# Decode kernel on one core: K and V in transfers of four batches, P^T by 32x32 transposes, w3 earlier, w4 in six pieces

## The chip, the core and the metric

The kernel runs on one core of a Trainium2 chip, alone. The metric is device time in microseconds. The core has TensorE (PE, with its weight loads listed apart as PEld), VectorE (DVE), ScalarE (ACT), GpSimd (POOL) and SyncE (SP), and 16 DMA engines that all queues share. In this kernel SP issues nearly every transfer.

## What is computed

The reference, cut to what matters (all data bf16, B = 4, one query position, D = 576, 32 query heads and 16 kv heads of 128, a window of W = 2048 keys, F = 4608):

```python
xn = layernorm(x)
q  = xn' @ wq                                   # xn' is layernorm(x) as given to block A
s  = q . k[:, :, Sk-W:, :] / sqrt(128)          # two query heads share one kv head
o  = softmax(s) . v[:, :, Sk-W:, :]
A  = o @ wo
h  = gelu(layernorm(xn) @ w1)
hs = concat(shifted quarters of h along the sequence) @ w2    # sequence length 1: every shift gives zeros
x1 = xn + hs
B  = x1 + gelu(layernorm(x1) @ w3) @ w4
out = x + A + B
```

K and V are 33.5 MB each in the window, wq and wo 4.7 MB each, w3 and w4 5.3 MB each, w1 and w2 0.66 MB each: 88.5 MB, each byte read once.

## The kernel before, in words

Five instruction streams are written as lists of operations with a key; each list is sorted by key (L535) and emitted, with waits on named events. So the order on an engine is the order of keys. `KS`, `KV` and `KT` (L166 to L168) are the keys where softmax, PV and the tail begin.

*Transfers (SP).* wq goes first, in five transfers, into the space of the V ring. Then K in 32 units of 1 MB: a unit is one kv head and two of the four batches, 128 partitions with 8 KB each (L193). The K ring has 7 such slots, the V ring 9. A K unit waits for the transposes of the unit 7 before it (L203), a V unit for the PV of the unit 9 before it (L207). wo goes behind V unit 8, w1 and w2 behind V unit 10, all into the K ring once K is used up (`wo_wait`, L204). w3 (five transfers) and w4 (five) come last; w3 takes the place of the K^T buffers, w4 that of V slots.

*Scores.* For each kv head, TensorE transposes 64 K tiles of 128x128 against the identity in eight blocks of 8 (L324), ACT and DVE copy each block from PSUM to one of 12 buffers (L330, L331), and 16 products with 32 columns of weights each (L340) add the scores of two query heads and four batches into four PSUM banks, where all heads share 128 rows (batch by 32). These products come two blocks late (`SC_LAG`).

*Softmax and P^T.* One maximum over all 2048 columns (L360), eight exps of 64 partitions (L366), interleaved by batch into a zeroed buffer, 32 transposes on TensorE (L375), copies to `PT` (L382, L384).

*PV.* For each V unit, 32 products with V as weights and 4 columns of `PT` moving (L405). After 4, 7 and 8 of 8 groups of heads (`AO_CH`, L437), the finished columns are scaled by the row sums (L440), reordered by a product with columns of the identity (L419), copied (L444) and multiplied with wo into two PSUM accumulators (L426 from L434).

*Block B.* hs, x1, its layernorm and gelu(h) run between PVs (keys from `KH`, L455). The products with w3 (L501 to L511) and gelu follow all PVs, the products with w4 (L426 from L524) follow those; the two halves of the output are copied on DVE and ACT and stored.

Of the kernel before, what the change touches and what calls it, by code (L numbers as in the profile page):

```python
# [12 lines left out]
NKU = 7  # L13
NVU = 9
NKT = 12
NTB = 3
# [3 lines left out]
WO_AFTER = 9  # L20
W12_AFTER = 11
AO_CH = ((0, 4), (4, 7), (7, 8))

# [13 lines left out]
def bass_parallel_sum__sliding_block_cached__mixer_s_mlp__decode_kernel(  # L37
# [9 lines left out]
    NU = 2 * G  # L47
    NT = 32
    UE = NT * 128
    NHB = 4 * NU  # L50
# [8 lines left out]
    with ExitStack() as ctx:  # L59
# [28 lines left out]
        assert _o <= NKU * UE  # L88
# [19 lines left out]
        ident_bf = sb("ident_bf", [128, 128], BF16)  # L108
        ident_f = sb("ident_f", [128, 128], FP32)
# [9 lines left out]
        P_sb = sb("P_sb", [128, NT, 64, 2], BF16)  # L119
        PT = sb("PT", [128, NT, 128], BF16)  # L120
# [8 lines left out]
        PTps = [ps[:, 4 + k, :].bitcast(BF16).rearrange("p (t r) -> p t r", t=8) for k in range(4)]  # L129
# [38 lines left out]
        KT = KV + NU + 8.0  # L168
# [9 lines left out]
        P(lambda e: e.memset(P_sb[:], 0.0), sig="p_zero", key=-95)  # L178
# [14 lines left out]
        def kv_pairs(ring_t, slot, cache, u):  # L193
            g, pr = u // 2, u % 2
# [3 lines left out]
        def last_unit(nslots, s_lo, s_hi):  # L198
            return max(u for u in range(NU) if s_lo <= u % nslots <= s_hi)

        for u in range(NU):
            ev_k.append(add_dma(kv_pairs(kring_t, u % NKU, A_k_cache, u), ("k", u % NKU),
                                [f"T{4 * (u - NKU) + 3}"] if u >= NKU else [], u))  # L203
        wo_wait = f"T{4 * last_unit(NKU, 0, (_o - 1) // UE) + 3}"  # L204
        for u in range(NU):
            kk = KS + 0.01 * u
            w = [f"PV{u - NVU}"] if u >= NVU else (["q"] if u < WQ_SLOTS else [])  # L207
            ev_v.append(add_dma(kv_pairs(vring_t, u % NVU, A_v_cache, u), ("v", u % NVU), w, kk))
            if u == WO_AFTER - 1:
                wo_d = wo_sb.rearrange("p h r n -> p h (r n)")  # L210
                wo_s = A_wo.rearrange("(h p r) n -> p h (r n)", h=8, r=4)
                wo_8 = A_wo.rearrange("(h a p r) n -> h a p (r n)", h=8, a=8, r=4)
                ev_wo = add_dma([(wo_d[:, 0:6, :], wo_s[:, 0:6, :])] + [(wo_d[:, h, :], wo_8[h]) for h in (6, 7)],
                                "wo", [wo_wait], kk + 0.005)
            if u == W12_AFTER - 1:
                ev_w1 = add_dma([(w1main, B_w1[0:512, :].rearrange("(p r) n -> p r n", r=4)), (w1rag, rag_src(B_w1))], "w1",
                                [wo_wait], kk + 0.005)
                ev_w2 = add_dma([(w2main, B_w2[0:512, :].rearrange("(p r) n -> p r n", r=4)), (w2rag, rag_src(B_w2))], "w2",
                                [wo_wait], kk + 0.006)
        w3_src = B_w3[0:512, :].rearrange("(p r) n -> p r n", r=4)  # L220
        ev_w3 = [add_dma([(w3main[:, r, :], w3_src[:, r, :])], ("w3", r), [f"SC{G - 1}"], KT + r) for r in range(4)]
        ev_w3.append(add_dma([(w3rag, rag_src(B_w3))], ("w3", 4), [f"SC{G - 1}"], KT + 4))
        w4_main = B_w4[0:4096, :].rearrange("(c p r) n -> p c (r n)", p=128, r=4)
        w4_t3 = B_w4[4096:4480, :].rearrange("(p r) n -> p (r n)", r=3)
        w4_t1 = B_w4[4480:4608, :]
        w4tile = {}
        ev_w4 = []
        s4 = (NU - NVU) % NVU
        assert all((s4 + s_) % NVU + 2 <= NVU for s_ in (0, 2, 4))
        W4P = [(0, 3, 0), (3, 6, 2), (6, 8, 4)]  # L230
        for n, (c0, c1, s_) in enumerate(W4P):
            o0 = (s4 + s_) % NVU * UE
            v = vring_t[:, o0:o0 + (c1 - c0) * 4 * D].rearrange("p (c rn) -> p c rn", c=c1 - c0)
            ev_w4.append(add_dma([(v, w4_main[:, c0:c1, :])], ("w4", n), [f"PV{NU - NVU + s_ + 1}"], KT + 5 + n))
            for c in range(c0, c1):
                for q in range(4):
                    w4tile[4 * c + q] = v[:, c - c0, q * D:(q + 1) * D]
        o0 = (s4 + 4) % NVU * UE + 2 * 4 * D
        assert 2 * 4 * D + 4 * D <= 2 * UE
        v3 = vring_t[:, o0:o0 + 3 * D]  # L240
        v1 = vring_t[:, o0 + 3 * D:o0 + 4 * D]
        wl = [f"PV{NU - NVU + 5}"]
        ev_w4.append(add_dma([(v3, w4_t3)], ("w4", 3), wl, KT + 8))
        ev_w4.append(add_dma([(v1, w4_t1)], ("w4", 4), wl, KT + 9))
        for q in range(3):
            w4tile[32 + q] = v3[:, q * D:(q + 1) * D]
        w4tile[35] = v1
        W4N = [(12 * n, 12 * n + 12) for n in range(2)] + [(24, 32), (32, 35), (35, 36)]
# [69 lines left out]
        def pe_T(n):  # L318
            u, k = n // 4, n % 4

            def f(e):
                ins = None
                for t in range(8):
                    ins = e.transpose(tb[n % NTB][:, t, :], kring[:, u % NKU, 8 * k + t, :], ident_bf[:])  # L324
                return ins
            return f

        def evac(n):
            if n % 8 in ACT_EVAC:
                return "act", lambda e: e.activation(out=ktbuf[:, n % NKT], in_=tb[n % NTB], func=ACTF.Copy)  # L330
            return "dve", lambda e: e.tensor_copy(out=ktbuf[:, n % NKT], in_=tb[n % NTB])  # L331

        def pe_SC(g):
            def f(e):
                ins = None
                for c4 in range(4):
                    for b in range(B):
                        n = 8 * g + 4 * (b % 2) + c4
                        bh = b // 2
                        ins = e.matmul(Sps[32 * b:32 * b + 32, c4, :].rearrange("p (t i) -> p t i", t=8), lhsT=Qpad[:, g, b, :],  # L340
                                       rhs=ktbuf[:, n % NKT, :, bh:128:2],
                                       start=(g == 0), stop=(g == G - 1), tile_position=(0, 32 * b))
                return ins
            return f

        for n in range(NHB):
            w = [ev_k[n // 4]] if n % 4 == 0 else []
            if n == 0:
                w.append("ident_bf")
# [13 lines left out]
        for q in range(4):  # L363
            for bh in range(2):
                s = slice(64 * bh, 64 * bh + 64)
                add("act", lambda e, q=q, s=s, bh=bh: e.activation(  # L366
                    out=P_sb[s, 8 * q:8 * q + 8, :, bh], in_=Sps[s, q, :].rearrange("p (t i) -> p t i", t=8), func=ACTF.Exp,
                    bias=negb[s, 0:1], scale=scale, accum_out=rs4[s, q:q + 1]),
                    waits=["negb", "p_zero"], sig=f"exp{q}" if bh else None, key=KS + 0.1 + 0.01 * q + 0.001 * bh)

        def pe_PT(q):
            def f(e):
                ins = None
                for t in range(8):
                    ins = e.transpose(PTps[q][:, t, :], P_sb[:, 8 * q + t, :, :].rearrange("p i b -> p (i b)"), ident_bf[:])  # L375
                return ins
            return f
        for q in range(4):
            add("pe", pe_PT(q), waits=[f"exp{q}"] + ([f"E{NHB - 1 - k}" for k in range(NTB)] + ["xn2T"] if q == 0 else []),
                sig=f"PTt{q}", key=KS + 0.2 + 0.01 * q)  # L380
            if q == 3:
                add("act", lambda e: e.activation(out=PT[:, 24:32, :], in_=PTps[3], func=ACTF.Copy), waits=["PTt3"], sig="PT3", key=KS + 0.3)  # L382
            else:
                add("dve", lambda e, q=q: e.tensor_copy(out=PT[:, 8 * q:8 * q + 8, :], in_=PTps[q]), waits=[f"PTt{q}"],  # L384
                    sig=f"PT{q}", key=KS + 0.3 + 0.01 * q)
# [4 lines left out]
        add("pe", lambda e: e.matmul(rinvps, lhsT=ones_f[:], rhs=diag[:], start=True, stop=True), waits=["diag", "ones_f"],  # L390
# [6 lines left out]
        def pe_PV(u):  # L397
            g, pr = u // 2, u % 2
# [214 lines left out]
```

## Time and profile before

| | |
|---|---|
| time, median of 3 runs | 224.23 us (224.15 to 224.72) |
| profiled execution, first to last instruction | 223.5 us |
| HBM read | 88.49 MB, 396 GB/s over the span |
| TensorE busy | 162.7 us (73%) |
| DVE, ACT, POOL busy | 70.9, 62.1, 7.9 us |
| mean granted TensorE clock | 0.794 |

The profiled execution's span of 223.5 us is its own time between its first and last instruction; the timed runs' median is 0.7 us above it. In lines of groups the columns are: line, engine, operation, output <- input, shape, count, then busy time in us and mean ns of one, then idle time before it with what ended it. In the chain of waits a row is start, length, and what ran or was waited for.

### The profile page before, as it was taken

The page shows a single profiled execution, that of the slowest core. Times are in us where ns is not written, and L with a number is a line of the kernel's source. Part 1 is how long each engine was busy: PE and PEld are TensorE (multiplying, and loading weights), DVE is VectorE, ACT ScalarE, POOL GpSimd, SP SyncE. Part 2 cuts the span into 40 slices and gives each one's busy share as a digit, 9 for nine tenths or more (in the row PEclk, how much of TensorE's full clock was granted, in tenths as well). Part 3 has the DMA queues.
Part 4 walks back from the last instruction along what each step waited for, and adds up shares of the span by engine and source line. Part 5 has one row for each costly group of instructions (what it writes and reads, how often), then busy time and mean ns, then how long its engine had stood idle before and what let it go on. Part 6 is the DMA issues. An engine that isn't in the chain of part 4 may idle for free.

```text
span 223.5 us, 6245 instructions
## 1 busy us (share of the span) xinstructions
PE 162.7 (73%) x2934; PEld 124.7 (56%) x2934; DVE 70.9 (32%) x124; ACT 62.1 (28%) x76; POOL 7.9 (4%) x14
## 2 busy tenths in 40 slices
PE   0469999999999999997257731666974436977596
PEld 0457777777777777775047631544564335666263
DVE  5803565666666556664440000051000000000000
ACT  2001555555555555555594000001100000000000
POOL 8500000000000000000000000000000000000000
PEclk9999999999999999999855555555695555875579
DMA  6999999999999999999999999999999999999940
GB/s 250 424 421 421 418 422 421 418 425 416 416 424 418 418 424 419 422 416 419 419 417 407 415 411 418 419 422 419 419 419 418 421 419 421 422 413 408 411 177 1
DMA packets 13714, 88.91 MB, mean 398 GB/s; under 512 B 1388, under 2 KB 1784, under 8 KB 4472
## 3 DMA queue, kind: packets, MB, share of 16 engines
q1 hardware_dynamic: 13672, 88.50, 95.9%
q8 instruction: 23, 0.38, 0.7%
q14 instruction: 3, 0.02, 0.0%
q10 hardware_dynamic: 16, 0.01, 0.0%
HBM read 88.49 MB, written 0.00 MB: 396 GB/s over the span
## 4 chain that ended last, share of the span: by engine, by line
PE 47%; DMA 34%; ACT 12%; SPq 2%; issue 2%; DVE 1%
PE ps L324 23%; DMA vring<-in_A_v_cache_dram 15%; DMA vring<-in_B_w_dram 14%; PE ps L426 9%; ACT regB L330 8%; PE ps L340 8%; DMA vring<-in_A_wq_dram 5%; PE ps L405 5%; ACT P_sb L366 3%; SPq L159 2%; PE ps L312 1%; DVE rmax L360 1%; PE ps L375 0%; ACT PT L382 0%; PE ps L297 0%
## 5 line engine op out<-in xcount | busy, mean ns | idle before, releaser
L324 PE MATMUL ps<-ident_bf,kring 128*128 128x128 bf16 x1024 | 67.2, 222 | 0.4 <-ACT regB L330 0.2
L324 PEld LDWEIGHTS ps<-ident_bf,kring 128*128 128x128 bf16 x1024 | 58.5, 99 | 13.9 <-issue 7.3
L331 DVE COPY regB<-ps 128x1024 bf16<-128x1024 bf16 x80 | 52.3, 687 | 36.4 <-PE ps L324 34.6
L330 ACT ACTIVATE regB<-ps 128x1024 bf16<-128x1024 bf16 x48 | 47.5, 1022 | 48.4 <-PE ps L324 48.4
L405 PE MATMUL ps<-PT,vring 128*128 128x4 bf16 x1024 | 30.8, 166 | 29.9 <-DMA vring<-in_A_v_cache_dram 27.1
L405 PEld LDWEIGHTS ps<-PT,vring 128*128 128x128 bf16 x1024 | 29.0, 103 | 34.0 <-DMA vring<-in_A_v_cache_dram 28.8
L340 PE MATMUL ps<-regB,Qpad 128*32 128x512 bf16 x256 | 17.5, 392 | 4.5 <-ACT regB L330 4.5
L516 ACT ACTIVATE h2T_sb<-ps 128x144 bf16<-128x144 f32 x1 | 0.3, 291 | 49.6 <-PE ps L510 49.6
L426 PE MATMUL ps<-vring,h2T_sb 128*4 128x288 bf16 x72 | 11.9, 340 | 2.7 <-DMA vring<-in_B_w_dram 2.7
L440 DVE TENSOR_TENSOR OTn<-ps,rinvB 128x64 bf16<-128x64 f32 (+2 forms) x3 | 0.6, 202 | 38.5 <-PE ps L405 38.5
L340 PEld LDWEIGHTS ps<-regB,Qpad 128*32 128x32 bf16 x256 | 5.3, 94 | 11.1 <-ACT regB L330 5.9
L426 PE MATMUL ps<-kring,ORT 128*4 128x288 bf16 x64 | 11.0, 342 | 0.3 <-DVE ORT L444 0.3
L426 PEld LDWEIGHTS ps<-vring,h2T_sb 128*4 128x4 bf16 x72 | 7.1, 99 | 7.3 <-DMA vring<-in_B_w_dram 2.8
L262 ACT ACTIVATE sd<-mv 4x1 f32<-4x1 f32 x3 | 0.6, 202 | 35.0 <-DVE mv L260 35.0
L375 PE MATMUL ps<-ident_bf,P_sb 128*128 128x128 bf16 x32 | 4.1, 308 | 6.6 <-ACT P_sb L366 6.6
L531 DVE CAST out_sb<-ps 4x288 bf16<-4x288 f32 x1 | 0.4, 446 | 25.7 <-PE ps L426 25.7
L426 PEld LDWEIGHTS ps<-kring,ORT 128*4 128x4 bf16 x64 | 6.1, 99 | 4.4 <-DVE ORT L444 0.4
L478 DVE TENSOR_TENSOR x_bf<-ps,xn_bf 4x288 bf16<-4x288 f32 x2 | 0.9, 446 | 23.5 <-PE ps L473 23.5
L501 PE MATMUL ps<-x1nT,regB 128*128 128x4 bf16 x144 | 5.3, 172 | 3.0 <-DMA regB<-in_B_w_dram 2.9
L375 PEld LDWEIGHTS ps<-ident_bf,P_sb 128*128 128x128 bf16 x32 | 3.1, 138 | 7.9 <-ACT P_sb L366 7.9
L366 ACT ACTIVATE P_sb<-ps,negb 64x512 bf16<-64x512 f32 x8 | 6.6, 826 | 2.6 <-DVE negb L361 2.5
L276 PE MATMUL ps<-ident_bf,xn_bf 4*128 4x4 bf16 x8 | 0.5, 166 | 8.8 <-DVE ragsrc L269 8.4
(78 smaller groups left out, 69.7 us busy)
## 6 DMA issues: line engine op xcount, KB each, us to landing
kring<-in_A_k_cache_dram SPq DMA_DIRECT2D x32, 1024.0 KB, 12.1
vring<-in_A_v_cache_dram SPq DMA_DIRECT2D x32, 1024.0 KB, 21.2
regB<-in_B_w_dram SPq DMA_DIRECT2D x4, 1152.0 KB, 26.4
vring<-in_A_wq_dram SPq DMA_DIRECT2D x4, 1024.0 KB, 7.8
kring<-in_A_wo_dram SPq DMA_DIRECT2D x1, 3456.0 KB, 21.1
vring<-in_B_w_dram SPq DMA_DIRECT2D x2, 1728.0 KB, 30.9
kring<-in_A_wo_dram SPq DMA_DIRECT2D x2, 576.0 KB, 21.4
kring<-in_B_w_dram SPq DMA_DIRECT2D x2, 576.0 KB, 13.4
```

The costliest lines, as they stand in the source:

```text
L159: e.dma_start(o_, i_).then_inc(S[skey], 16)
L312: ins = e.matmul(ps[:, 4 + (w % NTB), :], lhsT=zeros_bf[:, 0:128], rhs=zeros_bf[:, :], start=True, stop=True)
L324: ins = e.transpose(tb[n % NTB][:, t, :], kring[:, u % NKU, 8 * k + t, :], ident_bf[:])
L330: return "act", lambda e: e.activation(out=ktbuf[:, n % NKT], in_=tb[n % NTB], func=ACTF.Copy)
L331: return "dve", lambda e: e.tensor_copy(out=ktbuf[:, n % NKT], in_=tb[n % NTB])
L340: ins = e.matmul(Sps[32 * b:32 * b + 32, c4, :].rearrange("p (t i) -> p t i", t=8), lhsT=Qpad[:, g, b, :], rhs=ktbuf[:, n % NKT, :, bh:128:2],
L360: add("dve", lambda e: e.tensor_reduce(out=rmax[:], in_=Sps, axis=AX.XY, op=ALU.max), waits=[f"SC{G - 1}"], sig="rmax", key=KS)
L366: add("act", lambda e, q=q, s=s, bh=bh: e.activation(out=P_sb[s, 8 * q:8 * q + 8, :, bh], in_=Sps[s, q, :].rearrange("p (t i) -> p t i", t ...
L375: ins = e.transpose(PTps[q][:, t, :], P_sb[:, 8 * q + t, :, :].rearrange("p i b -> p (i b)"), ident_bf[:])
L405: ins = e.matmul(o_, lhsT=vring[:, u % NVU, t, :], rhs=r_, start=(t == 0), stop=(t == NT - 1))
L426: return e.matmul(ACC[h], lhsT=lhsT, rhs=rhs, start=start, stop=stop)
L501: ins = e.matmul(H2Tps[:, n, :], lhsT=w3main[:, r, lo:hi:st], rhs=x1nT[:, r, :], start=(r == 0 and n == 0), stop=False, skip_group_check=True)
```

## The change

K and V units become one kv head with all four batches: 2 MB, 128 partitions with 16 KB each, partition = 4 x (position block) + batch. Both rings have four slots. The transposes of K go against a permuted identity (`perm_k`), so that K^T has its columns ordered by batch; there are 16 K^T buffers, and the score products read 16 pieces of 32 neighbouring columns. The softmax's exps take all 128 partitions, four in place of eight, and write P as it is. P^T is made by 32x32 transposes on DVE (`PTb`), a product with a second permutation (`perm_p`) and a copy (`PTs`); for each kv head a multiply on DVE spreads it over the batches with a mask (`PTg`, four buffers), and PV is 64 products of 8 columns for each kv head. The memset of P goes; two copies on POOL make the permutations, two small operations on DVE the mask.

wq goes in three transfers, wo in one. wo, w1 and w2 follow V of head 3; w3, in two transfers with its rows merged into one run per partition, follows V of head 6, and its products move between PV 6 and PV 7. w4 is laid out in 18 rows per partition and half, and goes in six pieces of 14, 4, 10, 4, 2 and 2 tiles that wait for PV 12, 13 and 14. The keys of block B are closer together (`KH`).

```diff
-NKU = 7
-NVU = 9
-NKT = 12
+NKS = 4
+NVS = 4
+NPG = 4
+NKT = 16
-WO_AFTER = 9
-W12_AFTER = 11
+WO_AFTER = 3
+W3_AFTER = 6
+W4P = ((0, 0, 14), (0, 14, 18), (1, 0, 10), (1, 10, 14), (1, 14, 16), (1, 16, 18))
...
-    NT = 32
+    NT = W // 32
...
-        P(lambda e: e.memset(P_sb[:], 0.0), sig="p_zero", key=-95)
+        P(lambda e: e.tensor_copy(out=perm_k[:].rearrange("p (b i) -> p b i", b=B), in_=ident_bf[:].rearrange("p (i b) -> p b i", b=B)),
+          waits=["ident_bf"], sig="perm_k", key=-95.5)
+        P(lambda e: e.tensor_copy(out=perm_p[:].rearrange("p (i b) -> p i b", b=B), in_=ident_bf[:].rearrange("p (b i) -> p i b", b=B)),
+          waits=["ident_bf"], sig="perm_p", key=-95)
...
-        for r in range(4):
-            ev_wq.append(add_dma([(wqmain[:, r, :], wq_src[:, r, :])], ("wq", r), (), -20 + r))
+        for r in (0, 2):
+            ev_wq += 2 * [add_dma([(wqmain[:, r:r + 2, :], wq_src[:, r:r + 2, :])], ("wq", r), (), -20 + r)]
...
-                     cache[pr:B:2, g, Sk - W:Sk, :].rearrange("b (i t) d -> i b (t d)", t=NT))]
+                     cache[:, g, Sk - W:Sk, :].rearrange("b (i t) d -> i b (t d)", t=NT))]
+        for g in range(G):
+            ev_k.append(add_dma(kv_pairs(kring_t, g % NKS, A_k_cache, g), ("k", g % NKS),
+                                [f"T{8 * (g - NKS) + 7}"] if g >= NKS else [], g))
+        wo_wait = f"T{8 * (G - 2) + 7}"
+        for g in range(G):
+            kk = KS + g
+            w = [f"PV{g - NVS}"] if g >= NVS else (["q"] if g < WQ_SLOTS else [])
+            ev_v.append(add_dma(kv_pairs(vring_t, g % NVS, A_v_cache, g), ("v", g % NVS), w, kk))
+            if g == WO_AFTER:
+                ev_wo = add_dma([(wo_sb.rearrange("p h r n -> p h (r n)"), A_wo.rearrange("(h p r) n -> p h (r n)", h=8, r=4))],
+                                "wo", [wo_wait], kk + 0.1)
...
+            if g == W3_AFTER:
+                ev_w3 = add_dma([(w3main, B_w3[0:512, :].rearrange("(p r) n -> p r n", r=4)), (w3rag, rag_src(B_w3))], "w3",
+                                [f"SC{G - 1}"], kk + 0.1)
+        w4_src = B_w4.rearrange("(h p r) n -> h p r n", h=2, p=128)
+        RT = F // 256
+        w4_sb = vring_t[:, 0:2 * RT * D].rearrange("p (t n) -> p t n", n=D)
...
+        for n, (h, r0, r1) in enumerate(W4P):
+            t0, t1_ = h * RT + r0, h * RT + r1
+            lst = (t1_ * D - 1) // UE
+            ev_w4.append(add_dma([(w4_sb[:, t0:t1_, :], w4_src[h, :, r0:r1, :])], ("w4", n),
+                                 [f"PV{max(g for g in range(G) if g % NVS == lst)}"], KS + G + 0.1 * n))
...
-                    ins = e.transpose(tb[n % NTB][:, t, :], kring[:, u % NKU, 8 * k + t, :], ident_bf[:])
+                    ins = e.transpose(tb[n % NTB][:, t, :], kring[:, g % NKS, 8 * k + t, :], perm_k[:])
...
-                        ins = e.matmul(Sps[32 * b:32 * b + 32, c4, :].rearrange("p (t i) -> p t i", t=8), lhsT=Qpad[:, g, b, :],
-                                       rhs=ktbuf[:, n % NKT, :, bh:128:2],
+                        t0 = 8 * ((8 * g + 2 * c4) % NKT)
+                        ins = e.matmul(Sps[32 * b:32 * b + 32, c4, :].rearrange("p (t i) -> p t i", t=16), lhsT=Qpad[:, g, b, :],
+                                       rhs=kttile[:, t0:t0 + 16, b, :],
...
+            cs = slice(512 * q, 512 * q + 512)
+            add("act", lambda e, q=q, cs=cs: e.activation(out=P_sb[:, cs], in_=Sps[:, q, :], func=ACTF.Exp, bias=negb[:, 0:1], scale=scale,
+                                                          accum_out=rs4[:, q:q + 1]),
+                waits=["negb"], sig=f"exp{q}", key=KS + 0.1 + 0.01 * q)
+            add("dve", lambda e, cs=cs: e.transpose(PTb[:, cs], P_sb[:, cs]), waits=[f"exp{q}"], sig=f"PTb{q}", key=KS + 0.2 + 0.01 * q)
+            add("pe", lambda e, q=q, cs=cs: e.matmul(ps[:, q, :], lhsT=perm_p[:], rhs=PTb[:, cs], start=True, stop=True),
+                waits=[f"PTb{q}"] + (["perm_p", "xn2T"] if q == 0 else []), sig=f"PTp{q}", key=KS + 0.2 + 0.01 * q)
+            dst = PTs[:, 16 * q:16 * q + 16, :].rearrange("p t r -> p (t r)")
...
+        for g in range(G):
+            add("dve", lambda e, g=g: e.tensor_tensor(
+                out=PTg[:, g % NPG], in0=PTs[:, :, 2 * g:2 * g + 2].unsqueeze(2).to_broadcast([128, NT, B, 2]),
+                in1=bmask[:].unsqueeze(1).to_broadcast([128, NT, B, 2]), op=ALU.mult),
+                waits=[f"PTs{q}" for q in range(4)] + ["bmask"] if g < NPG else [f"PV{g - NPG}"], sig=f"PTg{g}",
+                key=KS + 0.4 + 0.01 * g if g < NPG else KV + g - NPG + 0.6)
...
-                    ins = e.matmul(o_, lhsT=vring[:, u % NVU, t, :], rhs=r_, start=(t == 0), stop=(t == NT - 1))
+                    ins = e.matmul(OTps(g)[:, 8 * g:8 * g + 8], lhsT=vring[:, g % NVS, t, :], rhs=PTg[:, g % NPG, t].rearrange("p b e -> p (b e)"),
+                                   start=(t == 0), stop=(t == NT - 1))
...
-            kk = KV + 4 * z - 1
+            kk = KV + 2 * z - 1
...
-            add("pe", pe_AO(a, z), waits=[f"ORT{n}"] + ([ev_wo, "t1acc"] if n == 0 else []), sig=f"AO{n}", key=kk + (0.4 if last else 2.4))
+            add("pe", pe_AO(a, z), waits=[f"ORT{n}"] + ([ev_wo, "t1acc"] if n == 0 else []), sig=f"AO{n}", key=kk + (0.4 if last else 1.4))
...
-        KH = KV + 11.5
+        KH = KV + 4.1
...
+        KW = KV + W3_AFTER + 0.5
         for r in range(5):
-            add("pe", pe_h2(r), waits=[ev_w3[r]] + (["x1nT", "gelu_h"] if r == 0 else []), sig=f"h2_{r}", key=KT + r)
+            add("pe", pe_h2(r), waits=[ev_w3] + (["x1nT", "gelu_h"] if r == 0 else []), sig=f"h2_{r}", key=KW + 0.01 * r)
```

More of the change, by code (lines that the diff above doesn't have):

```diff
@@ L222, in bass_parallel_sum__sliding_block_cached__mixer_s_mlp__decode_kernel @@
[L222 to L226, printed above, removed]
-        ev_w4 = []
[L228 to L248, printed above, removed]
+                                [wo_wait], kk + 0.3)
@@ L363, in bass_parallel_sum__sliding_block_cached__mixer_s_mlp__decode_kernel @@
         for q in range(4):
[L364 to L382, printed above, removed]
-            else:
-                add("dve", lambda e, q=q: e.tensor_copy(out=PT[:, 8 * q:8 * q + 8, :], in_=PTps[q]), waits=[f"PTt{q}"],
-                    sig=f"PT{q}", key=KS + 0.3 + 0.01 * q)
+            cs = slice(512 * q, 512 * q + 512)
@@ L389, in bass_parallel_sum__sliding_block_cached__mixer_s_mlp__decode_kernel @@
             waits=["rinv", "ident_f"], sig="diag", key=KS + 0.52)
-        add("pe", lambda e: e.matmul(rinvps, lhsT=ones_f[:], rhs=diag[:], start=True, stop=True), waits=["diag", "ones_f"],
+        add("dve", lambda e: e.tensor_reduce(out=bmask[:, :, 0], in_=ident_bf[:].rearrange("p (i b) -> p b i", b=B), axis=AX.X, op=ALU.add),
+            waits=["ident_bf"], sig="bmask0", key=-41)
+        add("dve", lambda e: e.tensor_copy(out=bmask[:, :, 1], in_=bmask[:, :, 0]), waits=["bmask0"], sig="bmask", key=-40.9)
+        add("pe", lambda e: e.matmul(rinvps, lhsT=ones_f[:], rhs=diag[:], start=True, stop=True), waits=["diag", "ones_f", "PTs3"],
             sig="rinvp", key=KV + 2.5)
@@ L441, in bass_parallel_sum__sliding_block_cached__mixer_s_mlp__decode_kernel @@
                                                            in1=rinvB[:, 16 * a:16 * z], op=ALU.mult),
-                waits=["rinvB", f"PV{4 * z - 1}"], sig=f"OTn{n}", key=kk + 0.2)
-            add("pe", pe_sel(a, z), waits=[f"OTn{n}"] + ([f"ORT{n - 1}"] if n else []), sig=f"sel{n}", key=kk + (0.3 if last else 1.3))
+                waits=["rinvB", f"PV{2 * z - 1}"], sig=f"OTn{n}", key=kk + 0.2)
+            add("pe", pe_sel(a, z), waits=[f"OTn{n}"] + ([f"ORT{n - 1}"] if n else []), sig=f"sel{n}", key=kk + 0.3)
             add("dve", lambda e, a=a, z=z: e.tensor_copy(out=ORT[:, :, a:z, :], in_=ORps[:, :, a:z, :]),
-                waits=[f"sel{n}"], sig=f"ORT{n}", key=kk + 1.4)
-            add("pe", pe_AO(a, z), waits=[f"ORT{n}"] + ([ev_wo, "t1acc"] if n == 0 else []), sig=f"AO{n}", key=kk + (0.4 if last else 2.4))
+                waits=[f"sel{n}"], sig=f"ORT{n}", key=kk + 0.35)
+            add("pe", pe_AO(a, z), waits=[f"ORT{n}"] + ([ev_wo, "t1acc"] if n == 0 else []), sig=f"AO{n}", key=kk + (0.4 if last else 1.4))
         def pe_t1(e):
@@ L452, in pe_t1 @@
             return ins
-        KH = KV + 11.5
-        add("pe", pe_t1, waits=["t1", "ident_f"], sig="t1acc", key=KH + 5.1)
+        KH = KV + 4.1
+        add("pe", pe_t1, waits=["t1", "ident_f", "PTs1"], sig="t1acc", key=KH + 2.2)
         def pe_hT(e):
@@ L512, in f @@
+                for n in range(2 * RT):
+                    h, k = n // RT, n % RT
+                    if r < 4:
+                        w, x_ = w3main[:, r, FH * h + k:FH * (h + 1):RT], x1nT[:, r, :]
+                    else:
+                        w, x_ = w3rag[:, k:FH:RT], x1nT[:, 4 + h, :]
+                    ins = e.matmul(H2Tps[:, n, :], lhsT=w, rhs=x_, start=(r == 0 and n == 0), stop=(r == 4), skip_group_check=True)
                 return ins
             return f
+        KW = KV + W3_AFTER + 0.5
@@ L521, in f @@
+        add("act", lambda e: e.activation(out=h2T_sb[:], in_=H2Tps, func=ACTF.Gelu_apprx_tanh), waits=["h2_4"], sig="gelu2", key=KW + 0.1)
+        last_p = len(W4P) - 1
+        for n, (h_, r0, r1) in enumerate(W4P):
+            def f(e, t0=RT * h_ + r0, t1_=RT * h_ + r1, hs=(0, 1)):
                 ins = None
```

120 lines of the change are left out of this document (40 added, 80 removed).

## The prediction

> **What bounds the kernel now.** I read the page first: the slices of the span and the transfer queues.
>
> ```profile
> span 223.5 us, 6245 instructions
> ...
> DMA  6999999999999999999999999999999999999940
> GB/s 250 424 421 421 418 422 421 418 425 416 416 424 418 418 424 419 422 416 419 419 417 407 415 411 418 419 422 419 419 419 418 421 419 421 422 413 408 411 177 1
> ...
> q1 hardware_dynamic: 13672, 88.50, 95.9%
> ```
>
> The 16 transfer engines are busy from the first slice to the last but two. Nothing that only shortens computation in the middle moves the end. Two things can: the time that 88.5 MB need, and what TensorE still has to do behind the last bytes. The end of the chain of waits shows the second, and busy time in half-microsecond windows shows when the transfers end (columns: window, its length, PE, weight loads, DVE, ACT, POOL, granted clock, DMA share, GB/s).
>
> ```profile
> 177.40 31.97 DMA vring<-in_B_w_dram
> 209.37 0.04 issue
> 209.41 11.91 PE ps L426 x72
> 221.32 0.02 issue
> 221.34 0.40 ACT out_sb L532
> ```
>
> ```profile
> 217.00:217.50 0.50, 0.50 (x7) 0.35 (x5) 0.00 (x0) 0.00 (x0) 0.00 (x0) 1.00 0.13 44
> 217.50:218.00 0.50, 0.50 (x7) 0.35 (x5) 0.00 (x0) 0.00 (x0) 0.00 (x0) 1.00 0.00 0
> ```
>
> The first third of w4 lands at 209.37. TensorE then runs all 72 products with w4 without a gap until 221.3, although the last bytes are there by 217.5. From 221.3 to the end of the span, 2.2 us go to the last copy and the store. So: transfers to 217.5, 3.8 us more of TensorE, 2.2 us of ending. The span is 223.5 us and the median of the runs 224.23, so I add 0.7 to a span; a change under 0.3% (0.7 us) could not be told from none.
>
> **Part 1: longer runs (gain).** K and V go from 8192 runs of 8 KB to 4096 of 16 KB. wq goes from 512 runs of 8 KB to 256 of 16 KB, the main part of w3 from 512 of 9 KB to 128 of 36 KB, w4 from 1280 runs (mostly 4.6 KB) to 768 (six pieces of 128). Per engine that is 256 + 16 + 24 + 32 = 328 packets fewer for the same bytes. What is a packet worth? I compare two stretches of the transfer view: 50 us of K alone (30 to 80), then 5 us of w4 (206 to 211).
>
> ```profile
> DMA packets 2872, 20.95 MB, mean 419 GB/s; under 512 B 321, under 2 KB 321, under 8 KB 321
> q1 hardware_dynamic: 2865, 20.84, 100.3%
> q8 instruction: 6, 0.10, 0.8%
> ```
>
> ```profile
> DMA packets 466, 2.05 MB, mean 411 GB/s; under 512 B 19, under 2 KB 19, under 8 KB 466
> q1 hardware_dynamic: 466, 2.05, 101.8%
> ```
>
> K: 16 engines x 50 us x 1.003 = 802 us for about 2544 packets of 8192 B, 315 ns each (313 with the instruction fetches' 0.8% taken off). w4: 16 x 5 x 1.018 = 81.4 us for 447 packets of 4608 B, 182 ns each. The slope is (313 to 315 - 182)/3584 B = 0.0366 to 0.0371 ns per B, and what is left over is 10 to 13 ns per packet. I take 12: 328 x 12 = **3.9 us**. No row shows a 16 KB run from these caches, so the ends are 0 (a run is cut in two) and 328 x 15 = 4.9 us (slope taken a little flatter); I take the fitted value: both stretches are saturated, and the fixed part is what separates 411 from 419 GB/s. With 37 transfers fewer, each with 16 small packets (the 321 above are 20 transfers x 16), some tenths more: I count 4.0 us.
>
> That 4.0 us count in full needs the engines never to run dry, so the rings matter.
>
> **Part 2: rings of four 2 MB slots (price 0 if they hold).**
>
> ```profile
> 2.83 11.46 DMA vring<-in_A_wq_dram
> ...
> 93.54 0.64 PE ps L324 x8
> ...
> 98.94 0.64 PE ps L324 x8
> ...
> 107.28 2.30 DVE rmax L360
> ...
> 109.80 0.87 ACT P_sb L366 x2
> ```
>
> ```profile
> L324 PE MATMUL ps<-ident_bf,kring 128*128 128x128 bf16 x1024 | 67.2, 222 | 0.4 <-ACT regB L330 0.2
> ...
> L501 PE MATMUL ps<-x1nT,regB 128*128 128x4 bf16 x144 | 5.3, 172 | 3.0 <-DMA regB<-in_B_w_dram 2.9
> ```
>
> ```profile
> 18.22 0.11 PEld L324 LDWEIGHTS ps<-ident_bf,kring 128*128 128x128 bf16 x1 [0.32 <-DMA kring<-in_A_k_cache_dram]
> ```
>
> (The chain of waits, two groups by line, and the first weight load of a K block in the timeline.) One kv head takes TensorE 98.94 - 93.54 = 5.40 us; its 2.1 MB take 5.0 us now and 4.9 with part 1. TensorE falls behind by half a microsecond per head. The first unit is twice as large, so transposes begin 1 MB / 419 GB/s = 2.5 us later than 18.2: at 20.7. Head g's 64 transposes take 67.2/16 = 4.2, so the last is done by 24.9 + 5.4 g. SP queues K of head g+4 then, and bytes flow about 1.5 us later (SP issues first at 0.8, and the 250 GB/s of the first slice put the first byte at 2.3): 26.4 + 5.4 g. The three units still queued last until 14.3 + 4.9 (g+4) = 33.9 + 4.9 g. The margin is 7.5 - 0.5 g, 2.0 us at g = 11, the last such wait. It holds, narrowly. V of heads 0 to 3, wo, w1 and w2 follow, waiting at most for the transposes of head 14 (101 us), while V lasts until 112.
>
> Next, V of head 4 waits for PV of head 0 (now PV covers four batches). The queue up to w2 holds wq 4.7 + K 33.6 + four V 8.4 + wo 4.7 + w1, w2 1.3 = 52.7 MB, which last until about 2.3 + 52.7/0.425 = 126 us. The path: scores end at 107.3 + 2.1 = 109.4; max and negation to 112.0; four exps of 0.87 instead of eight (the rows below: the time goes by columns, and the partitions were halved) to 115.5. Behind the last exp come a 32x32 transpose on DVE, a permuting matmul, a copy and a masked multiply, none of which the trace has; the nearest rows are these.
>
> ```profile
> L331 DVE COPY regB<-ps 128x1024 bf16<-128x1024 bf16 x80 | 52.3, 687 | 36.4 <-PE ps L324 34.6
> ...
> L366 ACT ACTIVATE P_sb<-ps,negb 64x512 bf16<-64x512 f32 x8 | 6.6, 826 | 2.6 <-DVE negb L361 2.5
> ...
> L312 PE MATMUL ps<-zeros_bf 128*128 128x512 bf16 x6 | 2.7, 630 | 0.0
> ...
> L481 DVE TENSOR_TENSOR t<-x_sb,x_bf 4x576 f32<-4x576 bf16 x1 | 0.7, 740 | 0.0
> ```
>
> Half a 1024-column copy (0.35) to the 0.74 of 576 columns for each DVE step, 0.63 for the matmul, 0.83 for the copy on ACT: 2.2 to 2.9 us. I take 2.8, so PV of head 0 starts at 118.3 and ends 64 x 28 ns = 1.8 us later, V of head 4 flows from about 122. Margin 4 us; price 0, and beyond 4 us each microsecond counts. In steady state a V slot is refilled with three units (14.6 us) queued and PV done some 4 us after landing; w3's products (180 of 5.3/144 = 37 ns, 6.6 us), now between PV 6 and 7, and the first wo block (32 products, at most 7.5 us by the prices below) behind PV 8 use up 7 of the remaining 10. Price 0. The mask products of later heads (0.74 us per 4.9 us) hide on DVE. The memset of P that goes (3.5 us on POOL) was beside wq's transfer: 0.
>
> **Part 3: the tail (gain near 0, from -2 to +2).** w4 waits for PV 12, 13 and 14, early enough: its queue is never empty. w3's products leave the tail, but in front of 209.4 they hid behind w4 anyway. What counts is TensorE behind V of head 14. For its products the windows of L426 alone (same columns, PE and weight loads only) and the rows of the last wo blocks:
>
> ```profile
> 188.44:191.50 3.06, 3.06 (x13) 1.61 (x14) 0.50 0.99 408
> 191.50:193.02 1.52, 1.52 (x12) 0.85 (x10) 1.00 1.06 442
> 209.40:215.40 6.00, 5.99 (x26) 3.17 (x27) 0.50 0.79 314
> 215.40:221.30 5.90, 5.90 (x48) 3.89 (x46) 1.00 0.13 51
> ```
>
> ```profile
> 192.96 1.75 PE L405 MATMUL ps<-PT,vring 128*128 128x4 bf16 x64
> ...
> 194.75 0.17 DVE L440 TENSOR_TENSOR OTn<-ps,rinvB 128x16 bf16<-128x16 f32 x1 [8.21 <-PE ps L405]
> ...
> 195.56 1.14 PE L426 MATMUL ps<-kring,ORT 128*4 128x288 bf16 x8 [0.28 <-DVE ORT L444]
> ```
>
> A 288-column product costs 0.235 us at clock 0.50 and 0.123 at 1.00; the clock rose after 3.1 us of such work in one place and 6.0 in the other. With transfers ending at 217.5 - 4.0 = 213.5 and w4 taking 5.31 MB / 0.418 = 12.7 us, V 15 lands at 200.8, V 14 at 195.9, the first w4 piece (14 of 36 tiles) 22/36 x 12.7 = 7.75 before the end, at 205.75. TensorE: PV 14 to 197.7, wo block (24 products, 4.6 as from 188.4 to 193.0) to 202.3, PV 15 to 204.1, scaling and reordering 0.8, last wo block (8 x 0.235 = 1.9) to 206.8. So w4's first piece waits a microsecond for TensorE, not the other way round. If the clock rises 4.5 us after 204.9 (the middle of 3.1 and 6.0), 11 of the 72 products are slow and 61 fast: 2.6 + 7.5 = 10.1, end 216.9, span 219.1, time **219.8**. The last pieces landing at 213.5 do not bind. The tail behind the transfers is 3.4 us, against 3.8 now: the smaller last pieces bring little, because TensorE has a backlog.
>
> **The rivals.**
> - *Warm tail.* The clock stays at 1.00 from the 24-product block on: wo 3.0 and 1.0, first piece at 205.75, third landing at 210.7, then 36 x 0.123 = 4.4 more: 215.2, span 217.4, time 218.1. For it: 191.5 to 195 shows 1.00 kept across a PV. Against: that clock had fallen again by 209.4.
> - *Packets cost (nearly) the same.* A 16 KB run takes what two of 8 KB took: all of part 1 falls away, 223.8; with a third of it left, 222.5. For it: no row shows such a run. Against: 182 ns and 313 to 315 ns leave 10 to 13 ns fixed. The Trainium skill, "DMA: Bandwidth & Descriptors", section "Why small descriptors are slow (HBM only)", has a fixed overhead of about 3 cycles per packet; at the 850 MHz that the same page gives for the fabric that would be an estimate of 3.5 ns, a third of what the two stretches show here, and so the 222.5.
> - *K ring runs dry (slower).* The margin at head 11 is 7.5 - 11 x (p - 4.9) for a period p: dry beyond p = 5.58, every 0.1 us more costs 1.1. Transposes against a permutation, and scores reading 32-column pieces in place of every second column, could lengthen p; it makes the kernel slower than before from p = 6.05. At p = 6.2 it loses 6.8 us: 226.6. For it: TensorE is already the slower side there. Against: same shapes, same counts.
> - *Four batches disturb the memory (slower).* Neighbouring partitions now read from four batches 32 MiB apart instead of two 64 MiB apart. Slower than before begins with K and V at about 416 GB/s; at 400 GB/s their 67.1 MB take 168 instead of 156 us, 232. For it, nothing in the trace: two batches ran at 419 in every slice, and all transfers lie on one line. The Trainium skill, same page, section "Latency and other measured facts", has rates of 103 to 207 GB/s for partitions at pitches of 512 KiB and more in powers of two; the 419 of before, with neighbours 64 MiB apart, speaks against it here.
>
> **How the numbers follow.** Forecast 0.52, at 219.8 (218.6 to 222.6: the lower end with 4.9 for part 1, the upper with the clock at 0.50 throughout the wo blocks and 6 us into w4). Warm tail 0.18, same packet cost 0.13, K ring 0.08, memory 0.04, smaller dry spells elsewhere 0.05. Faster by over 0.3%: 0.52 + 0.18 + a third of the third case and a little of the last = 0.76; within 0.3%: 0.10; slower: 0.14. The range goes from the warm tail with the full 4.9 (217.2) to the case of equal packets (223.8).
>
> **What would show it.** The K stage at 428 to 432 GB/s with about half the packets (part 1; 419 refutes it). The DMA slices full from 2.3 to about 208 with no dip at 75 to 90 us (K ring) nor at 122 to 130 (PV 0). The last transfer at 213 to 214, TensorE without a gap from V 14 on, the w4 products starting behind the last wo block. Wrong if the DMA share dips anywhere, or if the products take the first piece as it lands.

## The result and the profile after

The changed kernel takes 221.14 us (median of 9 runs, 220.44 to 223.5), the kernel before 224.23 us (9 runs); the ratio is 0.9886, 95% interval 0.9849 to 0.9923 (the two medians alone would give 0.9862). The forecast was 219.8, the range 217.2 to 223.8. The profiled execution after spans 218.9 us and belongs to a run of 220.9 us.

The page after, and the same 50 us of K in the transfer view:

```profile
span 218.9 us, 6148 instructions
...
PEclk9999999999999999999955555555555578555999
DMA  6999999999999999999999999999999999999970
GB/s 240 431 431 425 431 428 425 428 425 421 431 425 425 428 407 413 410 424 431 425 407 409 409 439 422 433 429 413 426 425 425 425 428 428 428 425 424 407 304 27
...
q1 hardware_dynamic: 7816, 88.50, 96.1%
```

```profile
DMA packets 1459, 21.28 MB, mean 426 GB/s; under 512 B 160, under 2 KB 160, under 8 KB 160
q1 hardware_dynamic: 1452, 21.17, 99.8%
```

The engines are busy from end to end as before, with 7816 packets in place of 13672, and K moves at 426 GB/s in place of 419. Windows show when the transfers end, and a short dip in the K stage (columns as before: ..., granted clock, DMA share, GB/s):

```profile
81.50:82.00 0.50, 0.50 (x16) 0.11 (x4) 0.00 (x0) 0.50 (x1) 0.00 (x0) 1.00 0.69 295
82.00:82.50 0.50, 0.50 (x11) 0.39 (x8) 0.00 (x0) 0.00 (x0) 0.00 (x0) 1.00 0.82 328
...
214.00:214.50 0.50, 0.50 (x7) 0.35 (x5) 0.00 (x0) 0.00 (x0) 0.00 (x0) 1.00 0.30 115
214.50:215.00 0.50, 0.50 (x7) 0.35 (x5) 0.00 (x0) 0.00 (x0) 0.00 (x0) 1.00 0.01 5
```

The last bytes land at 214.5, before at 217.5: 3.0 us earlier. TensorE's timeline of the tail, and the windows of the 24-product wo block and of the first half of the w4 products (`--source L407`: window, its length, PE, weight loads, granted clock, DMA share, GB/s):

```profile
197.70 1.87 PE L386 MATMUL ps<-PTg,vring 128*128 128x8 bf16 x64 [2.28 <-DMA vring<-in_A_v_cache_dram]
199.49 4.27 PE L407 MATMUL ps<-kring,ORT 128*4 128x288 bf16 x24
203.69 1.76 PE L386 MATMUL ps<-PTg,vring 128*128 128x8 bf16 x64
...
206.30 1.14 PE L407 MATMUL ps<-kring,ORT 128*4 128x288 bf16 x8 [0.28 <-DVE ORT L425]
207.41 4.57 PE L407 MATMUL ps<-vring,h2T_sb 128*4 128x288 bf16 x36
212.28 4.57 PE L407 MATMUL ps<-vring,h2T_sb 128*4 128x288 bf16 x36 [0.29 <-DMA vring<-in_B_w_dram]
```

```profile
199.50:201.90 2.40, 2.40 (x11) 1.29 (x12) 0.50 1.00 425
201.90:203.70 1.80, 1.80 (x15) 1.09 (x13) 1.00 0.95 401
...
207.41:211.98 4.57, 4.57 (x37) 2.98 (x36) 1.00 0.86 348
```

The clock rises at 201.9, inside the 24-product wo block, and stays: the 72 products with w4 take 2 x 4.57 us, where before they took 11.9. They end at 216.85, 2.3 us behind the transfers (3.8 before).

So the profile shows two gains: transfers 3.0 us earlier, and a tail 1.5 us shorter that hangs on the clock. The second depends on which execution was profiled: this one had the higher clock in its tail, and not all runs have it (e3).

### The profile page after: what moved, and what is told of

Read it like the earlier page. It is cut to its first block, busy times and chain, and to the rows that moved or that the text cites. A ratio compares the mean times of both kernels' runs of the same rounds, so it can differ in the third digit from the quotient of the medians.

```text
span 218.9 us, 6148 instructions
## 1 busy us (share of the span) xinstructions
PE 161.0 (74%) x2900; PEld 125.7 (57%) x2902; DVE 81.0 (37%) x145; ACT 58.1 (27%) x69; POOL 4.8 (2%) x15
## 3 DMA queue, kind: packets, MB, share of 16 engines
q1 hardware_dynamic: 7816, 88.50, 96.1%
## 4 chain that ended last, share of the span: by engine, by line
PE 48%; DMA 35%; ACT 9%; DVE 3%; issue 2%; SPq 1%; DVEq 0%
PE ps L308 24%; DMA regB<-in_B_w_dram 14%; DMA kring<-in_A_k_cache_dram 8%; ACT regB L315 8%; DMA vring<-in_B_w_dram 8%; PE ps L324 8%; PE ps L386 6%; DMA vring<-in_A_v_cache_dram 5%; PE ps L479 5%; PE ps L407 5%; SPq L165 1%; DVE PTb L352 1%; DVE rmax L344 1%; ACT P_sb L349 0%; DVE PTg L363 0%
## 5 line engine op out<-in xcount | busy, mean ns | idle before, releaser
L308 PE MATMUL ps<-perm_k,kring 128*128 128x128 bf16 x1024 | 67.8, 223 | 1.8 <-DMA kring<-in_A_k_cache_dram 1.5
L308 PEld LDWEIGHTS ps<-perm_k,kring 128*128 128x128 bf16 x1024 | 59.1, 100 | 15.0 <-issue 6.4
L386 PE MATMUL ps<-PTg,vring 128*128 128x8 bf16 x1024 | 29.3, 168 | 22.7 <-DMA vring<-in_A_v_cache_dram 18.7
L386 PEld LDWEIGHTS ps<-PTg,vring 128*128 128x128 bf16 x1024 | 28.2, 102 | 24.9 <-DMA vring<-in_A_v_cache_dram 19.1
L479 PE MATMUL ps<-x1nT,regB 128*128 128x4 bf16 x180 | 11.3, 201 | 8.2 <-DMA regB<-in_B_w_dram 8.2
L479 PEld LDWEIGHTS ps<-x1nT,regB 128*128 128x128 bf16 x180 | 11.2, 165 | 9.3 <-DMA regB<-in_B_w_dram 9.3
L363 DVE TENSOR_TENSOR PTg<-PTs,bmask 128x512 bf16<-128x512 bf16 x16 | 10.4, 684 | 11.3 <-PE ps L386 11.0
L407 PE MATMUL ps<-kring,ORT 128*4 128x288 bf16 x64 | 11.9, 361 | 0.3 <-DVE ORT L425 0.3
L407 PE MATMUL ps<-vring,h2T_sb 128*4 128x288 bf16 x72 | 9.1, 286 | 0.3 <-DMA vring<-in_B_w_dram 0.3
L407 PEld LDWEIGHTS ps<-kring,ORT 128*4 128x4 bf16 x64 | 6.5, 105 | 4.9 <-DVE ORT L425 0.4
L281 PE MATMUL ps<-xnT,vring 128*128 128x4 bf16 x160 | 4.6, 166 | 4.7 <-DMA vring<-in_A_wq_dram 4.7
L407 PEld LDWEIGHTS ps<-vring,h2T_sb 128*4 128x4 bf16 x72 | 6.0, 85 | 3.5 <-DMA vring<-in_B_w_dram 0.9
L281 PEld LDWEIGHTS ps<-xnT,vring 128*128 128x128 bf16 x160 | 4.4, 104 | 4.8 <-DMA vring<-in_A_wq_dram 4.8
```

Source lines behind the costliest of these rows:

```text
L281: ins = e.matmul(QTps[:, B * h:B * (h + 1)], lhsT=w, rhs=x_, start=(r == 0 and h == 0), stop=(r == 4), skip_group_check=True)
L308: ins = e.transpose(tb[n % NTB][:, t, :], kring[:, g % NKS, 8 * k + t, :], perm_k[:])
L363: add("dve", lambda e, g=g: e.tensor_tensor(out=PTg[:, g % NPG], in0=PTs[:, :, 2 * g:2 * g + 2].unsqueeze(2).to_broadcast([128, NT, B, 2]) ...
L386: ins = e.matmul(OTps(g)[:, 8 * g:8 * g + 8], lhsT=vring[:, g % NVS, t, :], rhs=PTg[:, g % NPG, t].rearrange("p b e -> p (b e)"), start=(t ...
L407: return e.matmul(ACC[h], lhsT=lhsT, rhs=rhs, start=start, stop=stop)
L479: ins = e.matmul(H2Tps[:, n, :], lhsT=w, rhs=x_, start=(r == 0 and n == 0), stop=(r == 4), skip_group_check=True)
```

## The experiments

All ratios are to the kernel before, run beside each on the same chip; the experiments ran on several chips, so differences of a few tenths between two rows are not safe.

| kernel | median us (lowest to highest) | ratio, 95% interval |
|---|---|---|
| changed | 221.14 (220.44 to 223.5) | 0.9886 (0.9849 to 0.9923) |
| e1: 8 KB runs | 224.75 (222.89 to 225.59) | 0.9996 (0.9967 to 1.0024) |
| e2: w3 early, in the kernel before | 224.56 (223.43 to 224.99) | 0.9997 (0.9978 to 1.0015) |
| e3: clock kept | 220.78 (220.62 to 221.12) | 0.9836 (0.9816 to 0.9857) |
| e4: w4 in two pieces | 223.14 (223.03 to 224.18) | 0.9945 (0.9929 to 0.9962) |
| e5: P^T transposes x3 | 222.9 (220.57 to 223.33) | 0.9910 (0.9875 to 0.9945) |
| e6: P^T transposes x7 | 232.12 (230.68 to 232.26) | 1.0340 (1.0309 to 1.0371) |
| e7: w3 late | 229.54 (229.11 to 229.93) | 1.0239 (1.0214 to 1.0265) |
| e8: tail reordered | 220.4 (219.96 to 222.71) | 0.9854 (0.9817 to 0.9891) |
| e9: reordered, more filling | 220.52 (219.95 to 221.83) | 0.9842 (0.9812 to 0.9872) |
| e10: K stage longer | 229.22 (228.23 to 230.59) | 1.0223 (1.0176 to 1.0270) |
| e11: clock kept, smaller first piece | 220.1 (220.0 to 220.31) | 0.9808 (0.9787 to 0.9830) |

**e1: the run length alone, undone.**

```diff
-            return [(ring_t[:, slot * UE:(slot + 1) * UE], cache[...].rearrange("b (i t) d -> i b (t d)", t=NT))]
+            s_ = cache[:, g, Sk - W:Sk, :].rearrange("b (i y t) d -> y i b (t d)", y=2, t=NT // 2)
+            return [(ring_t[:, slot * UE + y * (UE // 2):slot * UE + (y + 1) * (UE // 2)], s_[y]) for y in range(2)]
```

> The changed kernel with each 2 MB K or V transfer cut into two of 1 MB with 8 KB runs (same ring, same slot, same waits); all else stays. Theory (longer runs are the gain): the K stage falls from 426 to about 420 GB/s, the last transfer lands 2.1 to 2.9 us later, the time rises by 2 to 3 us over the changed kernel, to 222.5 to 224.5 us, close to the kernel before. Rival (the tail or w3's new place are the gain, run length is nothing): unchanged, 220.5 to 221.5 us.

K in the transfer view of e1, then the end of its transfers in windows:

```profile
DMA packets 2874, 20.96 MB, mean 419 GB/s; under 512 B 322, under 2 KB 322, under 8 KB 322
```

```profile
216.50:217.00 0.50, 0.50 (x6) 0.34 (x4) 0.00 (x0) 0.00 (x0) 0.00 (x0) 1.00 0.17 65
217.00:217.50 0.50, 0.50 (x7) 0.34 (x5) 0.00 (x0) 0.00 (x0) 0.00 (x0) 1.00 0.00 0
```

With 8 KB runs the rate is 419 again, the transfers end at 217, 2.5 us later than in the changed kernel, and the time is that of the kernel before. The layout, the P^T path, w3's place and the pieces give nothing on balance without the long runs. (e1 also adds 32 transfers, each with its 16 small packets; no run parts these from the run length.) The theory held; only its median lies a quarter of a microsecond above the stated range.

**e2: w3 early, in the kernel before.**

```diff
-ev_w3 = [... KT + r) for r in range(4)]              # and KT + 4 for the rest
+ev_w3 = [... KS + 0.155 + 0.001 * r) for r in range(4)]    # and KS + 0.159
-            ... sig=f"h2_{r}", key=KT + r)
+            ... sig=f"h2_{r}", key=KV + 17.7 + 0.01 * r)   # gelu2: KV + 17.8
```

> The kernel before with w3 transferred behind V unit 15 and its products and gelu placed behind PV unit 17; all else of the kernel before stays, w4's five pieces too. Theory (w3's products were hidden behind w4's first piece, and that piece's landing starts the tail): no change, 223.7 to 224.7 us. Rival (w3 out of the tail is a part of the gain): 1.5 to 3 us less, 221 to 222.5 us.

No change. In the kernel before, w3's products end at 206.7 and TensorE then waits 2.7 us for w4's first piece: they were covered. In e2's profile V of the last head comes later instead, the last wo block stands in the place of w3's products, and the w4 products start behind it, at 210.3 against 209.4.

**e3: is it the clock?** The changed kernel's nine runs lie at 220.4 to 221.1 (five, mean granted clock 0.805 or 0.806) and at 222.5 to 223.5 (four, 0.792 to 0.799).

```diff
+        def pe_keep(n):      # n products of 512 columns, perm_p and PTs, into bank 3
...
+        for k_, n_ in ((KV + 10.95, 10), (KV + 11.95, 10), (KV + 12.95, 10), (KV + 13.95, 10), (KV + 15.1, 4), (KT + 19.9, 5)):
+            add("pe", pe_keep(n_), key=k_)
```

> The changed kernel plus products whose result nobody reads (ten of 512 columns ahead of each of PV 11 to 14, four behind PV 15, five ahead of the w4 products, 512 columns each into a free PSUM bank), so that TensorE has dense work before the tail. Theory (the changed kernel's runs near 220.6 and near 222.8 differ by the granted clock in the tail): all runs at 219.8 to 220.8 us, none near 222.8; the w4 products cost 0.123 us each throughout. Rival (the two groups have another cause, such as transfer speed): two groups stay, and the added work costs 0 to 2 us.

The same products alone in windows (wo, wo, w4):

```profile
199.40:202.50 3.10, 3.10 (x24) 1.96 (x24) 1.00 1.01 427
205.76:206.90 1.14, 1.14 (x8) 0.59 (x8) 1.00 0.88 366
208.02:217.00 8.98, 8.98 (x72) 6.03 (x72) 1.00 0.45 179
```

The upper group is gone, the clock is 1.00 in all three, and the 49 added products cost about 0.1 us against the lower group's median of 220.65. (Two of the five runs lie above the stated range, at 220.9 and 221.1; the five last products push the start of the w4 products from 207.4 to 208.0.) The other side shows in the profiled execution of e5 below. It has the changed kernel's tail and, at 223.33 us, is one of an upper group:

```profile
199.61 5.67 PE L409 MATMUL ps<-kring,ORT 128*4 128x288 bf16 x24
...
209.27 10.19 PE L409 MATMUL ps<-vring,h2T_sb 128*4 128x288 bf16 x72
```

```profile
214.50:215.00 0.50, 0.50 (x6) 0.34 (x4) 0.00 (x0) 0.00 (x0) 0.00 (x0) 1.00 0.05 18
```

Its transfers end within half a microsecond of the changed kernel's, but the wo block takes 5.67 us in place of 4.27 and the w4 products 10.19 in place of 9.14, and they end 2.6 us later. What parts the runs is the clock in the tail, not the speed of the transfers.

**e4: two pieces of w4.** `W4P = ((0, 0, 18), (1, 0, 18))`.

> The changed kernel with w4 in two pieces of 18 tiles in place of six. Theory: the first 36 products start with the first piece (18 tiles, 1.4 us later than 14), the other 36 only behind the last byte, so the end is the last transfer plus 4.4 us at clock 1.00 in place of plus 1.9: 2 to 3 us more, 222.7 to 224 us where the clock is up. Rival (the number of pieces does not matter, since TensorE has a backlog): 220.5 to 221.5 us.

```profile
208.57 4.57 PE L407 MATMUL ps<-vring,h2T_sb 128*4 128x288 bf16 x36 [0.95 <-DMA vring<-in_B_w_dram]
214.73 4.57 PE L407 MATMUL ps<-vring,h2T_sb 128*4 128x288 bf16 x36 [1.59 <-DMA vring<-in_B_w_dram]
```

Both pieces are waited for, the second until 214.7, when the last transfer is in, with 4.57 us of products behind it: 2.0 us more than six pieces by the medians, 2.5 against the changed kernel's lower group, whose clock in the tail was up as it is here. The number of pieces matters once the clock is up.

**e5 and e6: is P^T hidden, and how far?** The transposes of P on DVE are repeated, each waiting for the one before (n = 3, n = 7).

```diff
-            add("dve", lambda e, cs=cs: e.transpose(PTb[:, cs], P_sb[:, cs]), ...
+            for j in range(n):
+                add("dve", lambda e, cs=cs: e.transpose(PTb[:, cs], P_sb[:, cs]), ...
```

> The changed kernel with each of the four 32x32 transposes of P done three times in a row, the same result each time (0.68 us each, so PV of head 0 ends 5.5 us later, at about 124.7 us). Theory (softmax and P^T are hidden behind V of heads 0 to 3, wo, w1 and w2, which last until about 128 us): no change, 220.4 to 221.2 us or the 222.5 to 223.5 us of the low clock. Rival (P^T is on the path that sets the end): 5 us more, 225.5 to 228 us.

> The same with each transpose seven times (16.6 us more, PV of head 0 ends at about 136 us). Theory: V of head 4 is asked for 8 to 10 us after the queue has run dry, and all of that is lost: 228.5 to 232 us, with a hole in the transfers from about 128 to 137 us. Rival (the rings give it back later): under 224 us.

Three times costs nothing that can be told apart: its runs (220.57 to 223.33) lie where those of the changed kernel do, though the upper ones are more. Seven times empties the queue; windows of e6:

```profile
120.00:126.00 6.00, 0.61 (x1) 0.10 (x1) 5.76 (x9) 0.60 (x1) 0.00 (x0) 0.50 1.02 407
126.00:128.00 2.00, 0.44 (x1) 0.10 (x1) 1.93 (x4) 0.00 (x0) 0.00 (x0) 0.50 0.73 279
128.00:137.00 9.00, 2.93 (x83) 2.29 (x83) 8.47 (x16) 1.88 (x2) 0.00 (x0) 0.50 0.03 11
```

From 128 to 137 nearly nothing moves, and the kernel is 11 us slower (a tenth above the stated range): a hole in the transfers is not given back.

**e7: w3 late in the changed kernel.** `if g == G - 1:` for w3's transfers, `KW = KT + 10.0`.

> The changed kernel with w3 transferred behind V 15 and its products behind the last wo block, ahead of the w4 products, as in the kernel before; layout and pieces stay. Theory (in the changed layout the 180 products with w3 take 11.3 us, twice those of before, so they no longer fit behind w4's transfer): w3 lands at 202.5, its products end at 214, the 72 products with w4 follow at the low clock: 226 to 229 us. Rival (the place of w3 does not matter, as in the kernel before): 220.5 to 223.5 us.

```profile
202.40 11.32 PE L479 MATMUL ps<-x1nT,regB 128*128 128x4 bf16 x180 [7.65 <-DMA regB<-in_B_w_dram]
214.19 11.79 PE L407 MATMUL ps<-vring,h2T_sb 128*4 128x288 bf16 x72 [0.47 <-ACT h2T_sb L485]
```

8.4 us more than the changed kernel, half a microsecond above the range. The times of both blocks are as expected. So w3's early place gains nothing over the kernel before (e2), but the new layout cannot do without it.

**e8 and e9: the order of the tail.** The 24-product wo block ahead of PV 14, w4 in pieces of 10, 8, 8, 6, 2, 2 tiles, unread products ahead of PV 11, 12, 13 and 15 (e8), and three more behind PV 15 (e9).

> A version meant to beat both: the changed kernel with products nobody reads ahead of PV 11, 12 and 13 (ten of 512 columns each) and PV 15 (nine), the 24-product wo block ahead of PV 14 instead of behind it, and w4 in pieces of 10, 8, 8, 6, 2 and 2 tiles. Theory (with the clock up, TensorE's backlog is what is left behind the transfers): the w4 products begin near 206.1 in place of 207.4, TensorE catches up with the transfers, the end is the last transfer plus 0.5 us: 219.0 to 220.0 us. Rival (the last transfer already sets the end): 220.4 to 221 us.

> The reordered tail once more, with three more unread products behind PV 15 and ten in place of nine ahead of it, so that the low-work stretch between PV 15 and the last wo block, in which the clock fell, is filled. Theory: the clock stays at 1.00, the w4 products start near 206.7 and run 8.9 us: all runs at 219.3 to 220.1 us. Rival (the order of the tail gives nothing once the clock is kept): 220.6 to 221.1 us, as with the clock alone.

Both missed: the lowest runs reach 220.0, the medians 220.4 and 220.5. In e8's profile:

```profile
205.14 2.08 PE L417 MATMUL ps<-kring,ORT 128*4 128x288 bf16 x8 [0.28 <-DVE ORT L435]
207.01 9.62 PE L417 MATMUL ps<-vring,h2T_sb 128*4 128x288 bf16 x72
```

The last wo block takes 2.08 in place of 1.14: the clock was at 0.50 for 3.4 us, from 204.9 to 208.3. Three products more did not mend it: in e9's profile TensorE is busy for 95% of the time from 200.25 to 205.5, and the clock falls at 205.5 all the same. Why it falls here and not in e3 or e11 stays open.

**e10: the K ring's margin.** Three products of zeros more per head, into bank 7.

> The changed kernel with three products of zeros more per kv head (512 columns into a free PSUM bank), so that a head takes TensorE 6.0 us in place of 5.35. Theory (the K ring of four slots has no margin left at 5.35: some engines ran dry for 0.5 us at 82 us): the refills of K slots come 7 us later by head 11, of which at most 2 are covered, and 4.5 to 7 us are lost: 225 to 230 us, with the transfers idle several times between 50 and 95 us. Rival (a longer K stage is hidden, since the transfers go on with V): 220.5 to 223.5 us.

The transfer rate of e10 by slices of 5.7 us:

```profile
GB/s 248 443 414 431 437 414 434 428 414 430 379 328 371 342 354 379 365 423 421 425 420 411 409 437 420 446 442 393 420 431 428 417 437 423 420 433 410 410 109 1
```

From 57 to 97 us the rate is 328 to 379. The queue of these 40 us in the transfer view, first in e10 and then in the changed kernel:

```profile
q1 hardware_dynamic: 985, 14.30, 93.7%
```

```profile
q1 hardware_dynamic: 1144, 16.65, 98.7%
```

0.65 us more per head costs 8 us in all. In the two profiles it is 9.1: the transfers end some 7 us later (221.5 against 214.5), and the other 2 come from the tail, where the clock is low as in e5 (10.2 us for the w4 products in place of 9.1). The K stage of the changed kernel has next to no margin; with seven smaller slots and a lower rate the kernel before had not shown such a dip.

**e11: what beats both.** e3 without its last five products, and with e8's pieces.

> The kernel of the kept clock without its last five unread products, and with w4 in pieces of 10, 8, 8, 6, 2 and 2 tiles; the order of the wo blocks as in the changed kernel. Theory (with the clock up, the w4 products can start behind the last wo block at 206.8 if a smaller first piece is there, and then run without a gap): 219.3 to 220.0 us in all runs, 0.8 to 1.3 us less than the kept clock alone. Rival (the last transfer or the clock sets the end again): 220.4 us or more.

```profile
206.72 4.57 PE L417 MATMUL ps<-vring,h2T_sb 128*4 128x288 bf16 x36
211.58 4.71 PE L417 MATMUL ps<-vring,h2T_sb 128*4 128x288 bf16 x36 [0.29 <-DMA vring<-in_B_w_dram]
```

The median is 220.1 us, a tenth above the range, with all runs within 0.3 us: 1.9% under the kernel before, and 0.7 us under e3. Two things differ from e3, the five products left out and the pieces; which of them gives the 0.7 was not tried.

## Why the prediction was right, step by step

*What bounds it* held: the experiments that took time from the transfers (e1, e6, e10) moved the end by about that much, e10 by 2 us more because of the clock. Three of the signs that the prediction had set are missed by a little: K at 426 GB/s (428 to 432), the last transfer at 214.5 (213 to 214), and a short dip at 82 us, where any dip was to count against it.

*Part 1* was right in kind and too large: 4.0 us forecast, 3.0 in the two profiles, 2.4 between e1 and the changed kernel (lower groups: 223.0 and 220.65; the upper ones, 225.2 and 222.9, differ by 2.3). The packet itself was right: 16 x 50 x 0.998 / 1292 packets = 618 ns, 12 less than two of 315. But packet times overlap a little (the queue's share was 100.3% and is 99.8%), so not all of the 12 ns is time of the engine: the rate gives 2.1 MB / 0.419 - 2.1 MB / 0.426, some 80 ns per eight packets saved or 10 ns each, and 2.6 us for K and V. In these 80 ns is also the one small packet per engine that a transfer brings. The queue has 5856 packets fewer, 366 per engine (328 were forecast, and the small ones of 37 transfers); at 80 ns for nine that would be 3.3 us, and with 0.6 us lost in the K ring, as below, 2.7 are left: an estimate from these rates, and close to what was measured. The rival with equal packets is out (e1). So is the memory rival: e1 reads four batches in runs of 8 KB at 419 GB/s, the rate of two batches before.

*Part 2* held but for the K ring, with two terms mis-sized. The K ring's margin at head 11 was put at 2.0 us; there is next to none. The term that failed is the end of head 0's transposes, put at 24.9 us. Measured it is 26.6: the 64 transposes of the first head take 5.9 us, not 4.2, and the chain of waits of the changed kernel shows TensorE held by a copy of ACT before the last eight:

```profile
24.89 1.03 ACT regB L315
...
25.97 0.64 PE ps L308 x8
```

With 26.6 and the measured period of 5.34 us my formula leaves 0.9 us at head 11, and for e10's period of 5.99 a loss of 6.2 (4.5 as I had it), near the 7 us by which the transfers ended later. The 0.9 is an average over the engines, and some ran dry: the slices from 77 to 93 us have 407 to 413 GB/s against 426, an estimated 0.6 us where I had a price of 0. The softmax path was right (PV of head 0 starts at 117.35, forecast 118.3; e5, e6). w3's products were put at 6.6 us from rows of weights at every 4th column; at every 18th they take 11.3, 63 ns each. The V ring's margin took it: the transfers run on at 415 to 422 GB/s beside these products.

*Part 3*: the w4 products start at 207.4 (206.8). The forecast's clock was the wrong one for five of nine runs: the tail was warm from 201.9 on, nearly the rival with 0.18, in the profiled execution too; in four runs it was not. V of head 14 was there at 197.7 (195.9), and the higher clock then made the two wo blocks 1.1 us shorter than forecast and the w4 products 0.7 (9.4 with a wait of 0.3, forecast 10.1). That their end, 216.85, fits the forecast 216.9, and the span of 218.9 the forecast 219.1, is luck: V of head 14 came 1.8 us later, and TensorE's products behind it took 1.8 us less.

*Around the span* I took 0.7 us, from one profiled execution and the median of other runs. A run's time is 1.7 to 2.0 above its own span in both kernels (220.9 and 218.9; 224.23 and 222.5 for the kernel before). The execution with 223.5 was thus probably a microsecond above a usual one. With 1.8 in place of 0.7 the forecast would have been 220.9, against 221.14 measured: this term is most of what the forecast of 219.8 missed.

## What to carry to other kernels

Where transfer engines are busy from end to end, count packets: a fixed part of some 10 ns in 315 was the gain here, undone by e1, and it shows from two stretches with different run lengths. With the gain in hand, ask two things: whether each ring still has a margin at its last refill, since coarser slots and faster transfers both eat it, and what TensorE's clock is in the tail, in more than one execution. And take a run's own span before adding what lies around it.

## What the runs showed of the hardware that I had not expected

The granted clock fell between dense stretches and came back only 2.4 us into the next one (199.5 to 201.9); 44 to 49 unread products in otherwise idle time held it and took the spread of the runs from 3 us to 0.3 to 0.5 (e3, e11). Weight loads with columns 18 elements apart took 63 ns per product, those 4 apart 37, both at clock 0.50; the layout was not tried alone. In e10 the idle time of the engines from 57 to 97 us, some 2 us, is less than what the transfers lost there: the packets of 16 KB also took longer, 687 ns against 622 in the changed kernel (16 x 40 us x 0.937 / 873 and 16 x 40 x 0.987 / 1016). Why stays open.
